# A four-pass exponential on VectorE, with a scaled copy of V made on GpSimd, in an attention kernel

## The chip, the cores and the metric

The kernel runs on one core of one Trainium2 chip. The metric is the device time of one execution in microseconds (us). The core has five engines that run their own instruction streams and meet at semaphores: TensorE (PE; its weight loads are shown as PEld), VectorE (DVE), ScalarE (ACT), GpSimd (POOL) and SyncE (SP, which only issues DMAs here).

## The reference

A residual layer: softmax attention with 16 heads of 28 columns, gated by a feed-forward branch. Both branches read the same normalised input.

```python
xn = _layernorm(x, axis=-1)                       # x: 1 x 2048 x 448
# attention
qkv = (xn @ wqkv).reshape(B, S, 3, 16, 28).transpose(2, 0, 3, 1, 4)
q, k, v = qkv[0], qkv[1], qkv[2]
p = softmax(einsum("bhqd,bhkd->bhqk", q, k) * 28 ** -0.5, axis=-1)
s = einsum("bhqk,bhkd->bhqd", p, v).transpose(0, 2, 1, 3).reshape(B, S, 448) @ wo
# feed-forward branch, 448 -> 1792 -> 448
h = gelu(xn @ w1 + b1)
g = silu(h @ w2 + b2)
out = x + s * g
```

## The kernel before

**Tiles.** Heads are handled in four head groups of four heads; a head takes 32 rows (28 and 4 of padding), so a head group fills 128 rows. Queries are handled in four chunks of 512, keys in 16 tiles of 128. A *block* is one head group with one chunk of queries; there are 16 blocks. Within a block a *tile* is the scores of one key tile (128 rows) against 512 queries of one head: 64 tiles in a block, 1024 in all, numbered by `m`. Four consecutive tiles (one key tile, four heads) are a *group*, numbered 0 to 255; block b has the groups 16b to 16b+15. In the last block the queries are cut: first half of the chunk, then a quarter and a quarter, so a tile there holds two or four key tiles side by side; `pieces` (line 1210) lists them.

**The main stream.** `p_scores` makes the scores of two or three tiles at a time (a unit) in PSUM banks of `ring`: three banks for one unit, two for the next, by turns. `p_exps` takes a unit's exponential on ScalarE (line 1293) into a slot of `P`, or, when they are free, of `h` and `xnT`. The scores of unit u wait until the exponential of unit u-2 is done. `p_pv` and `pv_task` multiply each exponential tile by the values (`vaug`, 28 columns and a column that yields the softmax's sum) and add the results of a block up in the PSUM bank `acc` (line 1508); four heads run beside each other in column strips of 32. At a block's end `p_epi` copies `acc` out (line 1566), and normalises by way of a reciprocal (line 1576), two small GpSimd instructions (lines 1578 and 1579), a product on PE (line 1588) and one on VectorE (line 1595). The next block's sums start in `acc` after the copy.

**The late groups.** `QUADS` (line 31) lists 35 groups whose exponential is not taken on ScalarE. Their scores go one tile at a time to whatever bank is free, alone or joined with a unit of the main stream (`p_late`), and VectorE writes from each tile a bfloat16 number whose bits are a scaled score (`p_apass`, line 1396): its exponent is the integer part of the score in base 2 and its mantissa the fraction, so that the tile T holds (1 + f) 2^e. `p_expq` corrects the fraction over all four tiles (128 x 2048) in five passes on VectorE:

- W keeps the mantissa under a fixed exponent (line 1447), so W = 2(1 + f);
- D1 = a W + b (line 1449);
- W = W D1 (line 1451);
- D1 keeps the exponent of T, 2^e (line 1452);
- W = W T (line 1454).

T, D1 and W are three of up to twelve *units* of memory that are free at the time (`x_sb`, `plx`, `w2`, `wq`, `wk`, `kT`). Their sum is the exponential; it isn't formed: `pv_task` multiplies all three by V, and PE adds them. So a late group costs three products with V where another costs one. One `p_expq` runs at a time (`K.ln2e`).

**Order.** The program is written by a planner: each process yields tasks with an engine, what they read and write, an estimated duration and a priority; `run` takes the task that can start first by the estimates and appends it to its engine's list, with the semaphore waits that `deps` derives. On the chip each engine runs its list strictly in order. `p_busy` adds products with a tile of zeros to `acc` (line 909) wherever the planner finds PE under 85% busy over 3.4 us.

**Other work.** Before and beside the main stream run the normalisation, the projections to q, k and v (lines 748 and 1039; v is written at line 1049), the first feed-forward product (line 1101), from block 8 the GELU (line 1150), then the second product (line 1171), the addition of `b2` on VectorE (line 1177), the gate (lines 1187 and 1191) and the output projection (lines 1605 and 1614). GpSimd issues the accumulating output DMAs (line 1622). All loads are issued by SP in the order of `loads`; `b2b`, a copy of `b2` for each partition, has a tile of its own.

Of the kernel before, what the change touches and what calls it, by code (L numbers as in the profile page):

```python
# [8 lines left out]
ALU = mybir.AluOpType  # L9
# [5 lines left out]
D = 448  # L15
# [4 lines left out]
C = 4  # L20
KT = 4
T = 16
# [5 lines left out]
MTOT = NBLK * T * 4  # L28

GM = 64 * 9 + 6  # L30
QUADS = (17, 18, 25, 37, 41, 58, 68, 70, 81, 90, 97, 98, 117, 124, 131, 135, 140, 142, 146, 154, 157, 159, 161, 162, 165, 183, 185, 197, 200, 210, 211, 225, 229, 234, 242)
SM_SCALE = DH ** -0.5
LOG2E = 1.4426950408889634
EXP_A3, EXP_A2, EXP_LC = 0.16391228, 0.00783292, 1.1187538523466403
EXP_OFF = 64.0 / (LOG2E * SM_SCALE)
LN_EPS = 1e-5
KNORM = 2.5
# [39 lines left out]
class _Kernel:  # L77
# [186 lines left out]
    def alloc(self):  # L264
        nc = self.nc
        f32, bf = dt.float32, dt.bfloat16
        sb = self.sb
# [27 lines left out]
        self.colK = sb("colK", [128, G], f32)  # L295
        self.plx = sb("plx", [128, 2048], bf)
        self.coff = sb("coff", [128, 1], f32)
        self.b2b = sb("b2b", [128, D], bf)
        self.st6 = sb("st6", [128, T, 6], f32)
        self.mv = sb("mv", [128, T, 2], f32)  # L300
        self.lnv = sb("lnv", [128, T], f32)
# [49 lines left out]
        self.b_qT = [[B() for _ in range(C)] for _ in range(G)]  # L351
        self.b_onT = self.b_qT
        self.q_ready = [[False] * C for _ in range(G)]
        self.b_v = [[B() for _ in range(T)] for _ in range(2)]
        self.b_h = [B() for _ in range(C)]
        self.b_g = [B() for _ in range(C)]
# [33 lines left out]
    def schedule(self):  # L390
        K = self
        K.n_f1 = 0
        K.exp_u = -1
        K.exp_m = -1
        K.late_ready = []
        K.sc_u = -1
        K.pv_m = -1
        K.E_done = -1
        K.norms_done = False
        K.stg_done = 0  # L400
        K.pe_wait = 0
# [12 lines left out]
        K.next_m = 0  # L414
        K.n_late = 0
        K.gu = None
        K.pend = None
        K.units = []
        K.pv_done = [False] * MTOT
        K.late = {4 * q + k for q in QUADS for k in range(4)}  # L420
        K.late_left = [sum(1 for q in QUADS if K.sub_of(4 * q) == b) for b in range(NBLK + 3)]
        K.late_on = False
        K.PB, K.PPREV, K.plast = {}, {}, {}
        K.free_u = []
        K.a_left = {}
        K.ln2e = 0
        K.late_blk = 0
        K.banks += [(K.ring[:, b, :], K.b_ring[b]) for b in (3, 2)]
        K.outs = []
        K.gelu_done = False  # L430
        K.dir_n = 0
        K.dir_read = 0
        self.constants()
        self.loads()
        for c in range(C):
            K.spawn(K.p_ln(c), c)
        K.spawn(K.p_first(), 0)
# [24 lines left out]
        for c in range(C):  # L462
            K.spawn(K.p_k(1, c), nxt())
        K.spawn(K.p_q(1, 0), nxt())
        for t in range(T):
            K.spawn(K.p_v1(t), nxt())
        for c in (1, 2, 3):
            K.spawn(K.p_q(1, c), nxt())
        K.spawn(K.p_qn(1), nxt())
        f1 = deque(SBT)  # L470
        for c in range(C):
            for _ in range(4):
                K.spawn(K.p_f1(*f1.popleft()), nxt())
            K.spawn(K.p_k(2, c), nxt())
            K.spawn(K.p_q(2, c), nxt())
        K.spawn(K.p_qn(2), nxt())
        while f1:
            K.spawn(K.p_f1(*f1.popleft()), nxt())
        for c in range(C):
            K.spawn(K.p_k(3, c), nxt())  # L480
            K.spawn(K.p_q(3, c), nxt())
        K.spawn(K.p_qn(3), nxt())
        K.spawn(K.p_gelu(), 0)
        K.spawn(K.p_direct(), 0)
        for c in range(C):
            for t in range(4):
                K.spawn(K.p_f2(c, t), nxt())
            K.spawn(K.p_silu(c), nxt())
        K.o_epi = 0.5
        for c in range(C - 1):  # L490
            for t in range(4):
                K.spawn(K.p_out(c, t), nxt())
        for t in range(4):
            K.spawn(K.p_last(t), nxt())
        K.run()
        for h in K.outs:
            K.wait(SP, h)
# [92 lines left out]
    def loads(self):  # L590
# [20 lines left out]
            ld(K.x_sb[:, c, :, :], xr[c], K.s_x[c], [K.b_x[c]], 8.0 + 1.8 * c)  # L611
        lw(4 * DH, D, K.s_wqk1, K.b_stg1, 16.5)

        ld(K.b2b[:, :], K.B_b2.partition_broadcast(128), K.s_w["b"], [K.b_b2], 20)
        ld(K.w1[:, 0:3, :], K.B_w1[0:384, :].rearrange("(kt p) f -> p kt f", p=128), K.s_w["w1"], [], 0)
        ld(K.w1[0:64, 3, :], K.B_w1[384:448, :], K.s_w["w1"], [K.b_w1], 30)

# [7 lines left out]
        def late_w2():  # L625
# [4 lines left out]
                    K.b_w2.r += b.r + [b.w]  # L630
            ld(K.w2[:, :, :], K.B_w2.rearrange("(ft p) d -> p ft d", p=128), K.s_w["w2"], [K.b_w2], K.now + 14)
        K.spawn(late_w2(), 50)

        def pool_pads():
            yield ("until", lambda: K.stg_done == 2)
# [525 lines left out]
    def p_f2(self, c, t):  # L1161
# [5 lines left out]
        for q in range(7):  # L1167
            def f(eng, q=q):
                ins = None
                for ft in (2 * q, 2 * q + 1):  # L1170
# [3 lines left out]
            yield _Task(PE, f, [K.b_w2, K.b_h[c]], [tok], 0.378, 0.17)  # L1174
        K.pe_wait -= 1
        fb = K.fsb[:, c % 2, t, :]
        yield _Task(DVE, lambda eng: eng.tensor_tensor(fb, ps, K.b2b[:, :], ALU.add), [tok, K.b_b2], [K.b_fsb[c % 2]],
                    0.63, 0.0, 2)
        K.banks.append((bank, tok))
        K.f2n[c] += 1  # L1180
# [251 lines left out]
    def p_expq(self, m0, u):  # L1432
        K = self
        b = K.sub_of(m0)
        uv = []
        yield ("until", lambda: K.ln2e == 0 and K.a_left[m0] == 0 and K.unit_of(b) is not None)
        K.ln2e = 1
        for _ in range(2):
            yield ("until", lambda: K.unit_of(b) is not None)
            v = K.unit_of(b)  # L1440
            K.free_u.remove(v)
            uv.append(v)
        K.late_blk = b
        u16, f16 = dt.uint16, dt.float16
        T, D1, W = K.unit[u], K.unit[uv[0]], K.unit[uv[1]]
        bT, bD, bW = K.b_U[u], K.b_U[uv[0]], K.b_U[uv[1]]
        yield _Task(DVE, lambda eng: eng.tensor_scalar(W.bitcast(u16), T.bitcast(u16), 0x407F, None, op0=ALU.bitwise_and),
                    bT, bW, 0.69, 0.0, 4)
        yield _Task(DVE, lambda eng: eng.tensor_scalar(D1.bitcast(f16), W, EXP_A3 / 4.0, EXP_A2 / 2.0, op0=ALU.mult, op1=ALU.add),
                    bW, bD, 0.69, 0.0, 4)  # L1450
        yield _Task(DVE, lambda eng: eng.tensor_tensor(W.bitcast(f16), W, D1.bitcast(f16), ALU.mult), bW + bD, bW, 1.22, 0.0, 4)
        yield _Task(DVE, lambda eng: eng.tensor_scalar(D1.bitcast(u16), T.bitcast(u16), 0x7F80, None, op0=ALU.bitwise_and),
                    bT + bW, bD, 0.69, 0.0, 4)
        yield _Task(DVE, lambda eng: eng.tensor_tensor(W, W.bitcast(f16), T, ALU.mult), bT + bW, bW, 1.22, 0.0, 4)
        K.ln2e = 0
        K.late_ready.append((m0, (u, uv[0], uv[1])))

    def p_pv(self):
        K = self
# [27 lines left out]
    def pv_task(self, q, late, ms):  # L1487
# [2 lines left out]
        for x in late:  # L1490
            K.late_ready.remove(x)
        K.late_left[b] -= len(late)
        src = [(m,) + K.p_slot(m) for m in ms if m not in K.late]
        for m0, us in late:
            for u in us:
                src += [(m0 + k, K.unit[u][:, 512 * k:512 * k + 512], K.b_U[u][k]) for k in range(4)]
        n = len(src) / 4
        fl, rd = [], []
        for kk in range(4):
            for m, ap, tok in src:  # L1500
                _, j, pc, _, s = K.pieces(m)
                g = q // 16 // C
                if kk >= len(pc):
                    continue
                t, q0, nq, col = pc[kk]

                def f(eng, t=t, j=j, g=g, q0=q0, nq=nq, col=col, ap=ap):
                    return eng.matmul(K.acc[32 * j:32 * j + 32, q0:q0 + nq], K.vaug[:, t, 4 * g + j, :],  # L1508
                                      ap[:, col:col + nq], tile_position=(0, 32 * j), start=(t == 0),
                                      stop=(t == T - 1), skip_group_check=True)  # L1510
                fl.append(f)
                rd += [tok, K.b_v[0 if g == 0 else 1][t]]

        if not src:
            return
# [1 line left out]
        def fall(eng, fl=fl):  # L1517
            ins = None
            for f in fl:
# [1 line left out]
            return ins  # L1521
        yield _Task(PE, fall, rd, [K.b_acc], 0.223 * n + 0.001 * len(fl), 0.17,
                    lambda: 1.2 if K.exp_m - K.pv_m > 20 or K.exp_m > MTOT - 12 or (K.gu is not None and K.gu - 1 <= K.exp_u <= K.gu) else 6, mode="col")
        for _, us in late:
            K.free_u += us

    def p_slot(self, m):
        i = self.PB[m]
# [170 lines left out]
```

## Time and profile before

| what | value |
|---|---|
| median of 4 runs | 459.8 us (459.69 to 460.25) |
| the profiled execution's own time | 460.08 us |
| its span, first to last instruction | 458.3 us |
| granted TensorE clock, mean | 0.998 of full speed |
| first exponential of the main stream starts | 12.99 us |
| end of block 0, 3, 7, 8, 11, 14 (copy of `acc`, line 1566) | 46.6, 128.3, 234.2, 274.8, 356.2, 432.6 us |

The page of the profile gives each engine's busy time, its share of the span and its number of instructions, then the busy share in 40 equal slices of the span as digits (9 is 90% or more). A group of instructions is named by the line of the kernel that issues it, the engine, the operation, what is written and read, the shape and the count; behind the first bar stand its busy time in us and the mean duration of one in ns, behind the second the idle time of its engine just before it and what ended most of that. A table of waits has who waited, for whom, the sum in us, the times and the longest. A window has its length and then busy time and count of PE, PEld, DVE, ACT and POOL, the clock, the DMA share and GB/s. Durations of neighbours on one engine can overlap by some 0.1 us.

### The profile page before, as it was taken

The page shows a single profiled execution, that of the slowest core. Times are in us where ns is not written, and L with a number is a line of the kernel's source. Part 1 is how long each engine was busy: PE and PEld are TensorE (multiplying, and loading weights), DVE is VectorE, ACT ScalarE, POOL GpSimd, SP SyncE. Part 2 cuts the span into 40 slices and gives each one's busy share as a digit, 9 for nine tenths or more (in the row PEclk, how much of TensorE's full clock was granted, in tenths as well). Part 3 has the DMA queues.
Part 4 walks back from the last instruction along what each step waited for, and adds up shares of the span by engine and source line. Part 5 has one row for each costly group of instructions (what it writes and reads, how often), then busy time and mean ns, then how long its engine had stood idle before and what let it go on. Part 6 is the DMA issues. An engine that isn't in the chain of part 4 may idle for free.

```text
span 458.3 us, 10703 instructions
## 1 busy us (share of the span) xinstructions
PE 437.6 (95%) x4475; PEld 164.5 (36%) x4475; DVE 381.6 (83%) x593; ACT 445.3 (97%) x406; POOL 44.9 (10%) x85
## 2 busy tenths in 40 slices
PE   6999999999999999999999999999999999999995
PEld 5543334332233233223234333333233333343562
DVE  8956988885878888968899899889878798889865
ACT  5999999999999999999999999999999999999994
POOL 7471000000000100100000001010000100111012
PEclk9999999999999999999999999999999999999999
DMA  8701000000000000000040000000000000402012
GB/s 270 268 2 37 2 0 1 1 1 4 1 0 1 1 2 2 3 1 1 0 139 5 2 0 1 2 1 1 0 1 2 1 1 1 82 1 33 11 23 62
DMA packets 8050, 11.16 MB, mean 24 GB/s; under 512 B 1698, under 2 KB 6994, under 8 KB 7955
## 3 DMA queue, kind: packets, MB, share of 16 engines
q1 hardware_dynamic: 6850, 8.43, 5.9%
q0 software_dynamic: 864, 1.38, 2.3%
q8 instruction: 35, 0.57, 0.5%
q10 hardware_dynamic: 288, 0.69, 0.4%
q14 instruction: 13, 0.10, 0.1%
HBM read 8.61 MB, written 3.21 MB: 26 GB/s over the span
## 4 chain that ended last, share of the span: by engine, by line
PE 55%; ACT 31%; issue 11%; DVE 2%; POOL 1%; ACTq 0%; DVEq 0%; POOLq 0%
PE ring L1237 16%; ACT P L1293 14%; PE acc L1508 9%; ACT xnT L1293 7%; ACT h L1293 7%; PE ring L1101 6%; PE ring L1171 4%; PE acc L909 4%; PE ring L748 3%; PE misc L1101 2%; PE misc L748 2%; PE misc L1039 1%; ACT h L1150 1%; PE misc L1171 1%; PE acc L891 1%
## 5 line engine op out<-in xcount | busy, mean ns | idle before, releaser
L1293 ACT ACTIVATE P<-ring 128x1024 bf16<-128x1024 f32 (+1 forms) x186 | 214.9, 1270 | 1.4 <-PE ring L1237 1.3
L1237 PE MATMUL ring<-qT,kT 32*128 32x512 bf16 (+2 forms) x1075 | 145.4, 358 | 10.9 <-ACT P L1293 3.9
L1293 ACT ACTIVATE h<-ring 128x1024 bf16<-128x1024 f32 (+1 forms) x103 | 118.5, 1244 | 0.4 <-PE ring L1237 0.2
L1237 PEld LDWEIGHTS ring<-qT,kT 32*128 32x128 bf16 x1075 | 37.5, 91 | 133.0 <-ACT P L1293 52.7
L1293 ACT ACTIVATE xnT<-ring 128x1536 bf16<-128x1536 f32 (+1 forms) x71 | 82.4, 1285 | 0.1
L1508 PE MATMUL acc<-P,vaug 128*32 128x512 bf16 (+2 forms) x526 | 48.4, 356 | 0.0
L1101 PE MATMUL ring<-xnT,w 128*128 128x512 bf16 x164 | 43.1, 382 | 0.2 <-ACT h L1150 0.2
L1578 POOL CAST rhi<-rc 128x16 bf16<-128x16 f32 x15 | 5.9, 393 | 357.6 <-DVE rc L1576 333.7
L1171 PE MATMUL ring<-w,h 128*128 128x448 bf16 x154 | 37.4, 355 | 0.0
L909 PE MATMUL acc<-ident,zero 128*128 128x128 bf16 x429 | 35.0, 220 | 0.0
L909 PEld LDWEIGHTS acc<-ident,zero 128*128 128x128 bf16 x429 | 24.3, 98 | 15.4 <-issue 14.6
L1237 PE MATMUL misc<-qT,kT 32*128 32x512 bf16 (+1 forms) x77 | 28.7, 377 | 0.0
L1508 PE MATMUL acc<-h,vaug 128*32 128x512 bf16 x250 | 28.0, 384 | 0.0
L1396 DVE TENSOR_SCALAR x_sb<-ring 128x512 uint16<-128x512 f32 x26 | 17.9, 687 | 2.8 <-PE ring L1237 2.6
L1101 PEld LDWEIGHTS ring<-xnT,w 128*128 128x128 bf16 x164 | 12.3, 97 | 20.1 <-issue 7.7
L1508 PE MATMUL acc<-xnT,vaug 128*32 128x512 bf16 (+2 forms) x232 | 18.1, 333 | 0.0
L1508 PEld LDWEIGHTS acc<-P,vaug 128*32 128x32 bf16 x526 | 12.0, 94 | 16.0 <-issue 13.4
L1171 PEld LDWEIGHTS ring<-w,h 128*128 128x128 bf16 x154 | 11.2, 97 | 17.1 <-issue 10.3
L1566 DVE CAST E_sb<-acc 128x512 bf16<-128x512 f32 x15 | 10.4, 691 | 8.3 <-PE acc L1508 8.3
L1101 PE MATMUL misc<-xnT,w 128*128 128x512 bf16 x60 | 17.2, 383 | 0.0
L1396 DVE TENSOR_SCALAR kT<-misc 128x512 uint16<-128x512 f32 x20 | 13.8, 688 | 4.1 <-PE misc L1237 4.1
L1396 DVE TENSOR_SCALAR x_sb<-misc 128x512 uint16<-128x512 f32 x22 | 15.1, 686 | 2.4 <-PE misc L1237 2.1
(281 smaller groups left out, 686.1 us busy)
## 6 DMA issues: line engine op xcount, KB each, us to landing
w<-in_B_w_dram SPq DMA_DIRECT2D x1, 1568.0 KB, 7.3
w<-in_B_w_dram SPq DMA_DIRECT2D x1, 1344.0 KB, 8.6
out_dram<-in_A_x_dram SPq DMA_DIRECT2D x3, 448.0 KB, 10.4
out_dram<-h POOLq DMA_DIRECT2D x6, 224.0 KB, 3.8
x_sb<-in_A_x_dram SPq DMA_DIRECT2D x2, 448.0 KB, 4.5
h<-in_A_wqkv_dram SPq DMA_DIRECT2D x3, 168.0 KB, 4.8
x_sb<-in_A_x_dram ACTq DMA_DIRECT2D x1, 448.0 KB, 4.1
h<-in_A_x_dram SPq DMA_DIRECT2D x1, 448.0 KB, 3.4
```

What stands on the lines that cost most here:

```text
L748: ins = eng.matmul(bank, w[:, kt, g * 128:(g + 1) * 128], K.xnT[:, kt, c * 512:(c + 1) * 512], start=(kt == 0), stop=(kt == KT - 1))
L891: yield _Task(PE, lambda eng: eng.matmul(bank[:, 0:256], K.ident[:, :], K.E_sb[:, 0, 0:256], start=True, stop=True), [K.b_id, K.b_pads], [ ...
L909: ins = eng.matmul(K.acc[:, 0:128], K.zero[:, :], K.ident[:, :], start=False, stop=True, skip_group_check=True)
L1039: ins = eng.matmul(bank[:, off:off + nh * 32], K.xnT[:, kt, t * 128:(t + 1) * 128], ap, start=(kt == 0), stop=(kt == KT - 1), skip_group_c ...
L1101: ins = eng.matmul(bank, K.w1[:, kt, ft * 128:(ft + 1) * 128], K.xnT[:, kt, c * 512:(c + 1) * 512], start=(kt == 0), stop=(kt == KT - 1))
L1171: ins = eng.matmul(ps, hv[:, ft, t * 128:(t + 1) * 128], K.w2[:, ft, :], start=(ft == 0), stop=(ft == FT - 1))
L1237: return eng.matmul(dst, K.kT[32 * j:32 * j + 32, g, t * 128:(t + 1) * 128], K.qT[32 * j:32 * j + 32, g, c * 512 + q0:c * 512 + q0 + nq], ...
L1293: return eng.activation(reg[:, i0:i0 + n, :], K.ring[:, b0:b0 + n, :], ACTF.Exp, scale=SM_SCALE)
L1396: yield _Task(DVE, lambda eng: eng.tensor_scalar(K.unit[u][:, 512 * k:512 * k + 512].bitcast(dt.uint16), bank, SM_SCALE * LOG2E * 128.0, ( ...
L1508: return eng.matmul(K.acc[32 * j:32 * j + 32, q0:q0 + nq], K.vaug[:, t, 4 * g + j, :], ap[:, col:col + nq], tile_position=(0, 32 * j), sta ...
L1566: yield _Task(DVE, lambda eng: eng.tensor_copy(E, K.acc[:, :]), [K.b_acc], [tE], 0.7, 0.0, 0)
L1578: yield _Task(POOL, lambda eng: eng.tensor_copy(K.rhi[:, :], K.rc[:, :]), [K.b_rc], [K.b_rhl], 1.1, 0.0, 1)
```

## The change

The exponential of the late groups becomes 2^e (1 + (1 + f) + C (1 + f)^3), with a cube in place of the quadratic and cubic terms, in four passes: W keeps the mantissa as before; D1 = W W; W = D1 T; D1 keeps the exponent of T. The factor C/4 isn't applied to the tiles: for each piece of a late group, GpSimd makes a copy of the four heads' values times C/4 (`p_cv`), 128 x 128, and the product of W with V takes the copy in place of `vaug`. There are four such copies (`cv`); a group's chain starts only when one is free and the values it copies are written. The list has 38 groups in place of 35, at other places for the most part: blocks 3, 11 and 12 have one more each, the other blocks as many as before.

To make room for `cv`, `b2b` is put into the memory of `wv` (the weights of v), and its load is issued by SP once all of v is written.

```diff
-QUADS = (17, 18, 25, 37, 41, 58, 68, 70, 81, 90, 97, 98, 117, 124, 131, 135, 140, 142, 146, 154, 157, 159, 161, 162, 165, 183, 185, 197, 200, 210, 211, 225, 229, 234, 242)
+QUADS = (17, 19, 21, 34, 41, 49, 53, 70, 74, 87, 88, 99, 108, 113, 114, 131, 135, 138, 141, 146, 149, 152, 157, 161, 162, 169, 177, 178, 184, 194, 195, 201, 212, 219, 226, 227, 236, 242)
...
-EXP_A3, EXP_A2, EXP_LC = 0.16391228, 0.00783292, 1.1187538523466403
+EXP_C, EXP_LC = 0.1669921875, 1.1155446
+NCV = 4
...
-        self.b2b = sb("b2b", [128, D], bf)
+        self.b2b = self.wv[:, 0, 0:D]
+        self.cv = sb("cv", [128, NCV, 128], bf)
...
-        ld(K.b2b[:, :], K.B_b2.partition_broadcast(128), K.s_w["b"], [K.b_b2], 20)
...
+        def late_b2():
+            yield ("until", lambda: all(x.tw is not None for x in K.b_v[1]))
+            K.b_b2.r += K.b_wv.r + K.b_wvpad.r + [K.b_wv.w, K.b_wvpad.w]
+            ld(K.b2b, K.B_b2.partition_broadcast(128), K.s_w["b"], [K.b_b2], K.now + 6)
+        K.spawn(late_b2(), 50)
...
-        yield ("until", lambda: K.ln2e == 0 and K.a_left[m0] == 0 and K.unit_of(b) is not None)
+        _, _, pc, _, _ = K.pieces(m0)
+        bv = K.b_v[0 if m0 // 64 < C else 1]
+        room = lambda: [i for i in range(0, NCV, len(pc)) if all(k in K.free_cv for k in range(i, i + len(pc)))]
+        yield ("until", lambda: K.ln2e == 0 and K.a_left[m0] == 0 and K.unit_of(b) is not None and room()
+               and all(bv[p[0]].tw is not None for p in pc))
         K.ln2e = 1
+        cs = list(range(room()[0], room()[0] + len(pc)))
+        for i in cs:
+            K.free_cv.remove(i)
+        g = m0 // 64 // C
+        K.spawn(K.p_cv(cs, [p[0] for p in pc], g, bv), m0)
...
-        yield _Task(DVE, lambda eng: eng.tensor_scalar(D1.bitcast(f16), W, EXP_A3 / 4.0, EXP_A2 / 2.0, op0=ALU.mult, op1=ALU.add),
-                    bW, bD, 0.69, 0.0, 4)
-        yield _Task(DVE, lambda eng: eng.tensor_tensor(W.bitcast(f16), W, D1.bitcast(f16), ALU.mult), bW + bD, bW, 1.22, 0.0, 4)
+        yield _Task(DVE, lambda eng: eng.tensor_tensor(D1.bitcast(f16), W, W, ALU.mult), bW, bD, 1.22, 0.0, 4)
+        yield _Task(DVE, lambda eng: eng.tensor_tensor(W, D1.bitcast(f16), T, ALU.mult), bT + bD, bW, 1.22, 0.0, 4)
         yield _Task(DVE, lambda eng: eng.tensor_scalar(D1.bitcast(u16), T.bitcast(u16), 0x7F80, None, op0=ALU.bitwise_and),
                     bT + bW, bD, 0.69, 0.0, 4)
-        yield _Task(DVE, lambda eng: eng.tensor_tensor(W, W.bitcast(f16), T, ALU.mult), bT + bW, bW, 1.22, 0.0, 4)
...
+    def p_cv(self, cs, ts, g, bv):
+        K = self
+        for i, t in zip(cs, ts):
+            yield _Task(POOL, lambda eng, i=i, t=t: eng.tensor_scalar(
+                K.cv[:, i, :], K.vaug[:, t, 4 * g:4 * g + 4, :].rearrange("p h e -> p (h e)"), EXP_C / 4.0, None, op0=ALU.mult),
+                [bv[t]], [K.b_cv[i]], 0.35)
...
+                w = K.vaug[:, t, 4 * g + j, :] if cs is None else K.cv[:, cs[kk], 32 * j:32 * j + 32]
...
-                rd += [tok, K.b_v[0 if g == 0 else 1][t]]
+                rd += [tok, K.b_v[0 if g == 0 else 1][t] if cs is None else K.b_cv[cs[kk]]]
```

More of the change, by code (lines that the diff above doesn't have):

```diff
@@ L353, in alloc @@
         self.q_ready = [[False] * C for _ in range(G)]
+        self.b_cv = [B() for _ in range(NCV)]
         self.b_v = [[B() for _ in range(T)] for _ in range(2)]
@@ L424, in schedule @@
         K.free_u = []
+        K.free_cv = list(range(NCV))
         K.a_left = {}
@@ L1176, in p_f2 @@
         fb = K.fsb[:, c % 2, t, :]
-        yield _Task(DVE, lambda eng: eng.tensor_tensor(fb, ps, K.b2b[:, :], ALU.add), [tok, K.b_b2], [K.b_fsb[c % 2]],
+        yield _Task(DVE, lambda eng: eng.tensor_tensor(fb, ps, K.b2b, ALU.add), [tok, K.b_b2], [K.b_fsb[c % 2]],
                     0.63, 0.0, 2)
@@ L1448, in p_expq @@
                     bT, bW, 0.69, 0.0, 4)
-        yield _Task(DVE, lambda eng: eng.tensor_scalar(D1.bitcast(f16), W, EXP_A3 / 4.0, EXP_A2 / 2.0, op0=ALU.mult, op1=ALU.add),
-                    bW, bD, 0.69, 0.0, 4)
-        yield _Task(DVE, lambda eng: eng.tensor_tensor(W.bitcast(f16), W, D1.bitcast(f16), ALU.mult), bW + bD, bW, 1.22, 0.0, 4)
+        yield _Task(DVE, lambda eng: eng.tensor_tensor(D1.bitcast(f16), W, W, ALU.mult), bW, bD, 1.22, 0.0, 4)
+        yield _Task(DVE, lambda eng: eng.tensor_tensor(W, D1.bitcast(f16), T, ALU.mult), bT + bD, bW, 1.22, 0.0, 4)
         yield _Task(DVE, lambda eng: eng.tensor_scalar(D1.bitcast(u16), T.bitcast(u16), 0x7F80, None, op0=ALU.bitwise_and),
                     bT + bW, bD, 0.69, 0.0, 4)
-        yield _Task(DVE, lambda eng: eng.tensor_tensor(W, W.bitcast(f16), T, ALU.mult), bT + bW, bW, 1.22, 0.0, 4)
         K.ln2e = 0
-        K.late_ready.append((m0, (u, uv[0], uv[1])))
+        K.late_ready.append((m0, (u, uv[0], uv[1]), cs))
+    def p_cv(self, cs, ts, g, bv):
[4 more added lines that the diff above has]
+                [bv[t]], [K.b_cv[i]], 0.35)
     def p_pv(self):
@@ L1492, in pv_task @@
         K.late_left[b] -= len(late)
-        src = [(m,) + K.p_slot(m) for m in ms if m not in K.late]
-        for m0, us in late:
+        src = [(m,) + K.p_slot(m) + (None,) for m in ms if m not in K.late]
+        for m0, us, cs in late:
             for u in us:
-                src += [(m0 + k, K.unit[u][:, 512 * k:512 * k + 512], K.b_U[u][k]) for k in range(4)]
+                src += [(m0 + k, K.unit[u][:, 512 * k:512 * k + 512], K.b_U[u][k], cs if u == us[2] else None) for k in range(4)]
         n = len(src) / 4
@@ L1499, in pv_task @@
         for kk in range(4):
-            for m, ap, tok in src:
+            for m, ap, tok, cs in src:
                 _, j, pc, _, s = K.pieces(m)
@@ L1505, in pv_task, with f @@
                 t, q0, nq, col = pc[kk]
-                def f(eng, t=t, j=j, g=g, q0=q0, nq=nq, col=col, ap=ap):
-                    return eng.matmul(K.acc[32 * j:32 * j + 32, q0:q0 + nq], K.vaug[:, t, 4 * g + j, :],
+                w = K.vaug[:, t, 4 * g + j, :] if cs is None else K.cv[:, cs[kk], 32 * j:32 * j + 32]
+                def f(eng, t=t, j=j, w=w, q0=q0, nq=nq, col=col, ap=ap):
+                    return eng.matmul(K.acc[32 * j:32 * j + 32, q0:q0 + nq], w,
                                       ap[:, col:col + nq], tile_position=(0, 32 * j), start=(t == 0),
@@ L1523, in pv_task @@
                     lambda: 1.2 if K.exp_m - K.pv_m > 20 or K.exp_m > MTOT - 12 or (K.gu is not None and K.gu - 1 <= K.exp_u <= K.gu) else 6, mode="col")
-        for _, us in late:
+        for _, us, cs in late:
             K.free_u += us
+            K.free_cv += cs
     def p_slot(self, m):
```

## The prediction

> **What bounds the kernel now.** I read the page's busy shares and slices first, to see which engine is full and where.
>
> ```profile
> span 458.3 us, 10703 instructions
> ...
> PE 437.6 (95%) x4475; PEld 164.5 (36%) x4475; DVE 381.6 (83%) x593; ACT 445.3 (97%) x406; POOL 44.9 (10%) x85
> ...
> DVE  8956988885878888968899899889878798889865
> ACT  5999999999999999999999999999999999999994
> ```
>
> ACT (ScalarE) is full in all slices but the first and the last. DVE (VectorE) stands at eight or nine tenths. The busy PE (TensorE) is not proof of a bound: 35.0 us of it are the products with `zero` of line 909, filler that the planner sets where it finds PE idle. So I asked for the busy time of the stretch between start-up and tail:
>
> ```profile
> 20.00:450.00 430.00, 419.04 (x4307) 152.87 (x4304) 359.83 (x528) 428.49 (x375) 30.49 (x50) 1.00 0.05 11
> ```
>
> After the length stand PE, weight load, DVE, ACT, POOL (GpSimd). ACT rests 1.5 us of 430; DVE rests 70.2. The chain of waits must agree, and at first sight it does not:
>
> ```profile
> PE 55%; ACT 31%; issue 11%; DVE 2%; POOL 1%; ACTq 0%; DVEq 0%; POOLq 0%
> ...
> PEld ring L1237 <- ACT P L1293: 52.7, 131, 0.7
> ```
>
> More than half of the chain is PE, but the second line, from the table of waits, says what PE waits for before scores: 131 times for an exponential to release the ring. With the same rows of tiles `h` (30.8) and `xnT` (21.3) that is 104.8 us. Scores and exponentials hand the same banks to and fro; the one that never rests, ACT, sets the pace. What a score tile costs ACT I read from its instructions in order of time:
>
> ```profile
> 98.89 1.46 ACT L1293 ACTIVATE P<-ring 128x1536 bf16<-128x1536 f32 x1
> 100.22 1.04 ACT L1293 ACTIVATE h<-ring 128x1024 bf16<-128x1024 f32 x1
> 101.13 6.01 ACT L1293 ACTIVATE P<-ring 128x1536 bf16<-128x1536 f32 x5
> ```
>
> Starts lie 1.33 us apart for three tiles and 0.91 for two, less than the durations, as neighbours overlap. Five tiles take 2.24 us: 0.448 per tile.
>
> **ScalarE's share.** There are 1024 tiles; 35 groups of four are VectorE's, so ScalarE has 884; with 38 groups it has 872. Twelve tiles by 0.448 are **5.4 us** off the full engine. A check from the whole: the stream from the first exponential (12.99) to its last (451.54) is 438.5; less 27.3 of GELU, 2.6 of table loads behind the first and 6.4 of tanh it leaves 402 us for 884 tiles, 0.455 each, or 5.5. I take 5.4.
>
> **VectorE's passes.** The rows of one group:
>
> ```profile
> L1396 DVE TENSOR_SCALAR kT<-misc 128x512 uint16<-128x512 f32 x20 | 13.8, 688 | 4.1 <-PE misc L1237 4.1
> L1451 DVE TENSOR_TENSOR kT<-kT,x_sb 128x2048 f16<-128x2048 bf16 x6 | 7.3, 1217 | 0.0
> L1454 DVE TENSOR_TENSOR kT<-kT,x_sb 128x2048 bf16<-128x2048 f16 x5 | 6.1, 1217 | 0.0
> L1452 DVE TENSOR_SCALAR x_sb<-w 128x2048 uint16<-128x2048 uint16 x7 | 4.8, 685 | 0.0
> L996 DVE TENSOR_TENSOR qsq<-qT 128x512 bf16<-128x512 bf16 x15 | 6.3, 419 | 0.4
> ```
>
> Before: four L1396 (2.75), three one-input passes L1447, L1449, L1452 at 0.69 (2.07), two products at 1.22 (2.44): 7.26 us. The new chain drops the pass of L1449 and keeps two products: 6.57. The new square of W has one tensor as both inputs; L996 is such a product, and (1217 - 419)/1536 = 0.52 ns per element joins the two sizes on one line, so I cost it at 1.22. In all 38 x 6.57 = 249.7 against 35 x 7.26 = 254.1: **4.4 us less work on VectorE**, though three groups more. It buys nothing by itself, as DVE rests; it is the room for the groups.
>
> **GpSimd's scaled copy.** 37 groups have one piece and group 242 two: 39 instructions of 128x128. No such row exists. From below, the copy of 128x128 (line 575) took 0.29; from above, the two-scalar form on f32 (line 567) 0.83. Between 128x4 (0.24, line 704) and 128x448 (0.76, line 714) a line gives 0.39, which I take as nearest in kind. That is 15.2 us on an engine that is busy 10%. The chain of a group now also waits for one of four free copies; as a group holds three of at most twelve units until it is added, four in flight are the most there were, and I cost this at nothing (a missing copy would cost a wait until an older group is added, on VectorE, which rests). The copy starts with the chain of passes, which needs 0.69 + 1.22 + 1.22 + 0.69 = 3.8 us before PE may use it. But GpSimd and VectorE do not run beside each other freely:
>
> ```profile
> L710 DVE TENSOR_SCALAR h<-x_sb,mv,rstd x10: 364/396/789, 6.0 to 27.2; 128x448 bf16<-128x448 bf16 x10
> ...
> L1578 POOL CAST rhi<-rc x15: 196/529/652, 49.8 to 434.7; 128x16 bf16<-128x16 f32 x15
> L1579 POOL TENSOR_TENSOR rlo<-rc,rhi x15: 217/543/1209, 50.1 to 435.3; 128x16 bf16<-128x16 f32 x15
> ```
>
> The numbers are shortest, median and longest. The 1.21 of L1579 at 183.82 began 0.09 after a VectorE product of 1.22 and ended with it; the 0.79 of L710 lay beside a GpSimd product of 0.93 and is twice its median. So a copy may wait 1.2 us and then hold a VectorE pass. Late: 1.2 + 0.39, with both lines 1578 and 1579 ahead of it in GpSimd's queue at their longest (1.86), 3.45 us, still under 3.8. From block 13 on an output DMA issue (line 1622, up to 1.18) can be ahead too; then PE waits 0.8 us at its products with the exponentials, and the next scores are queued behind them. Held: from 0, since around 183 the next VectorE pass began as usual, to 39 x 0.39 = 15.2 us of VectorE time, 3.4 points of its share.
>
> The Trainium skill, "SBUF — State Buffer", section "SBUF: two separate sides", says that the pair of ports which VectorE shares with GpSimd goes to one of them for a whole instruction, and that the other is blocked until it ends. It speaks against moving anything beside VectorE's passes. The rows agree in kind (0.79 against 0.40); by the rule taken to its end the upper bound of 15.2 us is the price on VectorE, by the rows around 183 nearly nothing.
>
> **TensorE.** A late group has three products with V for one: 24 more, at 0.76 us for 12 (the chain's pieces at line 1508) 1.5 us. Twelve scores leave the units for single ones: at most 12 x 0.22 = 2.6 (line 1508's sets of four start at 318.35, 318.56 and 318.78, and a score is as wide), less 12/2.5 = 4.8 units of 0.22: 1.1. Sum 3.0 us, half hidden under filler or more. Where filler lacks, ScalarE pays: bounds 0 to 3.0.
>
> **b2.** Its load leaves SP's queue at 8.22 (0.59 us of issue) and returns once the last v is written (line 1049, about 97 us), before the `qT<-qst` of 109. It took 6.2 us; its first reader, line 1177, comes at 281. Cost nothing; were that cover gone, 6.2 us.
>
> **Sum.** Profiled execution 460.08, span 458.3, median of the runs 459.8. The span becomes 458.3 - 5.4 = 452.9. For held passes and fuller PE I add 0.4, an estimate: ScalarE lost 1.5 us in 430 with VectorE at 83%, and I let that grow by a quarter. 453.3 of span, 455.1 for its own execution, and against the median **454.8 us**.
>
> **Rivals.** The three extra groups fall into blocks 3, 11 and 12 (the other changes shift groups within a block). The ends of the blocks are line 1566's copies; their windows:
>
> ```profile
> 102.10:128.30 26.20, 25.85 (x226) 7.39 (x224) 19.11 (x29) 26.18 (x24) 0.41 (x2) 1.00 0.01 3
> 331.30:356.20 24.90, 24.88 (x239) 8.24 (x235) 20.15 (x28) 24.90 (x22) 0.41 (x2) 1.00 0.01 2
> 356.20:380.80 24.60, 24.45 (x237) 8.21 (x234) 21.06 (x30) 24.55 (x22) 1.20 (x2) 1.00 0.01 1
> ```
>
> *TensorE takes over there.* For: filler in these blocks is 0.00, 0.68 and 1.19 us. Against: filler of 9.9 us in 402 to 433, to which the second feed-forward product (last at 386) can drift. All 3.0 us lost: 457.4.
>
> *VectorE becomes the bound in those blocks* and the sign turns. A block cannot end before its last group is added into `acc`, and PE stands in order there with the next scores behind it. Blocks 11 and 12 hold 41.2 us of VectorE; less 4 x 0.69, plus 2 x 6.57, that is 51.6 in 49.5 - 3.6 = 45.9 us: 5.7 too much. Block 3: 19.1 - 1.4 + 6.6 = 24.3 in 24.4, just full. Held passes of eight groups add 3.1. Price 8.8: **463.2 us**. It decides once more than 5.4 of this reaches ScalarE. Against: of blocks 11 and 12 some 10 us are other work (seven L1177 of 0.62, four L1191 of 1.09, two L1595 of 0.69), bound to no block's end; from 381 to 450 VectorE rests 11 us and is relieved of 4.
>
> *No change*: the passes become fewer but the plan leaves ScalarE 5.4 us of gaps through all blocks, 0.14 us per group: 459.8. Against: single waits of PE for VectorE before its products are at most 0.4 us.
>
> **How the numbers follow.** Forecast 0.60, TensorE 0.12, no change 0.06, VectorE bound 0.22. A measurement tells 0.2% (0.9 us) from no change: faster 0.72, within 0.05 (a near miss of either sign can pass it), slower 0.23. The low end: 454.4 less the 1.5 us ScalarE now rests is 452.9, so 453.0. Up to 457.4 the range covers the forecast and TensorE, and to 461.5 no change and a third of the last rival's cases: about 0.16 left out. The forecast's own range is 453.0 to 456.5.
>
> **What would show it.** ScalarE's exponentials must sum to 872 tiles and its rest between 20 and 445 stay under 2.5 us; a rest of 7 or more means that I am wrong, and its releaser says by whom: scores behind PE's line 1508 waiting for VectorE, or for GpSimd's copy. VectorE's busy time should fall to about 377 us; the square should take 1.22 us, the copy 0.39 alone and up to 1.6 when it waits. Passes of 0.69 that last 1.0 or more in the copies' shadow would prove the upper bound of the hold. Line 1177 should shift later than 386 by some us.

## The result, and the profile after

The kernel after takes **460.89 us** (median of 30 runs, 460.30 to 461.42) against 459.81 before (48 runs): a ratio of 1.0022, 95% interval [1.0017, 1.0027]. The forecast was 454.8, faster; it is 1.1 us slower. The profiled execution took 460.89.

First the page after, its busy shares and the slices of the two engines that were read before; then the stretch of 430 us:

```profile
span 459.4 us, 10832 instructions
PE 437.2 (95%) x4505; PEld 166.0 (36%) x4505; DVE 374.5 (82%) x582; ACT 440.9 (96%) x401; POOL 76.6 (17%) x124
...
DVE  8956898979678698789788988388988988798955
ACT  5999999999999999999999999999999999999992
```

```profile
20.00:450.00 430.00, 418.73 (x4339) 154.54 (x4337) 352.37 (x516) 425.13 (x371) 61.65 (x88) 1.00 0.05 11
```

VectorE has less to do (352.4 of 430 us, before 359.8), ScalarE too, but the last exponential ends only 0.9 us sooner (450.73, before 451.65): ScalarE's rest in this stretch grew from 1.5 to 4.9 us, between the two marks of the prediction (under 2.5 if right, 7 or more if wrong). The page says who ended it. Busy time and mean stand behind the first bar, the rest just before behind the second; first the kernel before, then after:

```profile
L1293 ACT ACTIVATE P<-ring 128x1024 bf16<-128x1024 f32 (+1 forms) x186 | 214.9, 1270 | 1.4 <-PE ring L1237 1.3
L1293 ACT ACTIVATE h<-ring 128x1024 bf16<-128x1024 f32 (+1 forms) x103 | 118.5, 1244 | 0.4 <-PE ring L1237 0.2
L1293 ACT ACTIVATE xnT<-ring 128x1536 bf16<-128x1536 f32 (+1 forms) x71 | 82.4, 1285 | 0.1
```

```profile
L1302 ACT ACTIVATE P<-ring 128x1024 bf16<-128x1024 f32 (+1 forms) x186 | 214.3, 1261 | 2.2 <-PE ring L1246 1.0
L1302 ACT ACTIVATE h<-ring 128x1024 bf16<-128x1024 f32 (+1 forms) x101 | 116.5, 1233 | 1.8 <-PE ring L1246 1.0
L1302 ACT ACTIVATE xnT<-ring 128x1536 bf16<-128x1536 f32 (+1 forms) x68 | 79.6, 1286 | 0.6 <-PE ring L1246 0.2
```

The exponentials (line 1293 before, 1302 now) waited 4.6 us, before 1.9, and where the page names what ended a wait it is scores (line 1237 before, 1246 now). The chain of waits, with more of TensorE in it (67%, before 55%), and the table of waits show the other side:

```profile
PE 67%; ACT 22%; issue 7%; DVE 3%; POOL 1%; ACTq 0%; DVEq 0%; POOLq 0%
```

```profile
PEld ring L1246 <- ACT P L1302: 50.4, 127, 0.8
PEld ring L1246 <- ACT h L1302: 30.8, 74, 0.7
...
PEld ring L1246 <- ACT xnT L1302: 15.9, 40, 1.3
```

TensorE waited for an exponential 241 times (97.1 us); before 256 times (104.8). Five of the 15 fewer go with the five units fewer; in the rest TensorE is no longer the one that waits.

**Where the time went.** I cut each profiled execution in three: up to the first exponential, from there to the end of the last (the stream), and the rest up to the execution's own time. In the stream I sum the spacing of two starts on ScalarE less 1.333 us behind an exponential of three tiles and less 0.906 behind one of two ("late starts"; shorter spacings count as negative), and take GELU's 17 instructions from the first start to the start of what follows them.

| kernel | start | stream | end | late starts | GELU |
|---|---|---|---|---|---|
| before | 13.0 | 438.7 | 8.4 | 8.1 | 25.3 |
| after | 13.1 | 437.7 | 10.2 | 11.5 | 26.1 |

The start is not a difference of the kernels: over all profiles here it lies between 12.5 and 13.2 us.

Five units are gone, two of three tiles and three of two: 2 x 1.333 + 3 x 0.906 = 5.4 us, just as forecast. Late starts gave back 3.4, and GELU 0.8, where its last instruction waits for a first feed-forward product (0.68 us); so the stream is only 1.0 shorter. Behind the last exponential 1.7 us were added. Put down to the blocks by the copies of `acc` that end them in each kernel, 3.0 of these 4.2 us came in blocks 5, 6 and 7 and about 1 in block 9 (most of it GELU's), which have as many late groups as before; blocks 3, 11 and 12, which have one more each, lost 0.7 (1.2, if each exponential is counted to the block of its tiles). The other blocks together were 0.5 us shorter. The largest late starts follow exponentials that start at 180, 203.8, 222.5 and 228 (0.6 to 0.7 us each) and, within GELU, 273 (0.8). The first of them, first ScalarE, then TensorE (start, duration, instructions):

```profile
180.17 1.12 ACT L1302 ACTIVATE h<-ring 128x1024 bf16<-128x1024 f32 x1
181.70 1.45 ACT L1302 ACTIVATE h<-ring 128x1536 bf16<-128x1536 f32 x1 [0.41 <-PE misc L1246]
```

```profile
179.52 0.61 PE L1110 MATMUL ring<-xnT,w 128*128 128x512 bf16 x2
180.06 0.62 PE L1533 MATMUL acc<-h,vaug 128*32 128x512 bf16 x8
180.50 0.39 PE L1533 MATMUL acc<-x_sb,vaug 128*32 128x512 bf16 x4
180.72 0.39 PE L1533 MATMUL acc<-w,vaug 128*32 128x512 bf16 x4
180.93 0.39 PE L1533 MATMUL acc<-w,cv 128*32 128x512 bf16 x4
181.25 0.39 PE L1246 MATMUL ring<-qT,kT 32*128 32x512 bf16 x3
```

TensorE doesn't wait here. Two products of the feed-forward branch, eight with exponentials and the late group's twelve stand in its list ahead of the next scores, and ScalarE rests 0.41 us until these are there. The products with the scaled copy (`cv`) are the last of this row, but they wait for nobody. At the other three places of the stream a late group's products stand just ahead of the scores as well, and at none of the four does a product with zeros.

### The profile page after: what moved, and what is told of

Same layout as the page of the kernel before. It is cut to its first block, busy times and chain, and to the rows that moved or that the text cites. A ratio compares the mean times of both kernels' runs of the same rounds, so it can differ in the third digit from the quotient of the medians.

```text
span 459.4 us, 10832 instructions
## 1 busy us (share of the span) xinstructions
PE 437.2 (95%) x4505; PEld 166.0 (36%) x4505; DVE 374.5 (82%) x582; ACT 440.9 (96%) x401; POOL 76.6 (17%) x124
## 4 chain that ended last, share of the span: by engine, by line
PE 67%; ACT 22%; issue 7%; DVE 3%; POOL 1%; ACTq 0%; DVEq 0%; POOLq 0%
PE ring L1246 18%; ACT P L1302 15%; PE acc L1533 13%; PE ring L1110 7%; PE ring L1180 5%; ACT xnT L1302 4%; PE misc L1110 4%; PE ring L757 3%; ACT h L1302 3%; PE misc L1180 3%; PE acc L918 3%; PE misc L757 2%; PE misc L1048 1%; PE ring L1048 1%; PE ring L1631 1%
## 5 line engine op out<-in xcount | busy, mean ns | idle before, releaser
L1246 PE MATMUL ring<-qT,kT 32*128 32x512 bf16 (+2 forms) x1074 | 143.0, 358 | 10.2 <-ACT P L1302 4.6
L1302 ACT ACTIVATE h<-ring 128x1024 bf16<-128x1024 f32 (+1 forms) x101 | 116.5, 1233 | 1.8 <-PE ring L1246 1.0
L1302 ACT ACTIVATE xnT<-ring 128x1536 bf16<-128x1536 f32 (+1 forms) x68 | 79.6, 1286 | 0.6 <-PE ring L1246 0.2
L1477 POOL TENSOR_SCALAR cv<-vaug 128x128 bf16<-128x128 bf16 x39 | 30.6, 785 | 158.5 <-PE acc L1533 156.6
L1110 PE MATMUL ring<-xnT,w 128*128 128x512 bf16 x152 | 39.3, 381 | 0.0
L1180 PE MATMUL ring<-w,h 128*128 128x448 bf16 x126 | 29.9, 355 | 0.2 <-DVE rc L1602 0.2
L1533 PE MATMUL acc<-h,vaug 128*32 128x512 bf16 x245 | 28.1, 385 | 0.0
L1405 DVE TENSOR_SCALAR x_sb<-ring 128x512 uint16<-128x512 f32 x31 | 21.2, 685 | 4.9 <-PE ring L1246 4.8
L1180 PE MATMUL misc<-w,h 128*128 128x448 bf16 x98 | 23.9, 355 | 0.0
L1110 PE MATMUL misc<-xnT,w 128*128 128x512 bf16 x72 | 20.0, 382 | 0.0
L1405 DVE TENSOR_SCALAR x_sb<-misc 128x512 uint16<-128x512 f32 x25 | 17.1, 684 | 2.6 <-PE misc L1246 2.5
```

Source lines behind the costliest of these rows:

```text
L1110: ins = eng.matmul(bank, K.w1[:, kt, ft * 128:(ft + 1) * 128], K.xnT[:, kt, c * 512:(c + 1) * 512], start=(kt == 0), stop=(kt == KT - 1))
L1180: ins = eng.matmul(ps, hv[:, ft, t * 128:(t + 1) * 128], K.w2[:, ft, :], start=(ft == 0), stop=(ft == FT - 1))
L1246: return eng.matmul(dst, K.kT[32 * j:32 * j + 32, g, t * 128:(t + 1) * 128], K.qT[32 * j:32 * j + 32, g, c * 512 + q0:c * 512 + q0 + nq], ...
L1302: return eng.activation(reg[:, i0:i0 + n, :], K.ring[:, b0:b0 + n, :], ACTF.Exp, scale=SM_SCALE)
L1405: yield _Task(DVE, lambda eng: eng.tensor_scalar(K.unit[u][:, 512 * k:512 * k + 512].bitcast(dt.uint16), bank, SM_SCALE * LOG2E * 128.0, ( ...
L1477: yield _Task(POOL, lambda eng, i=i, t=t: eng.tensor_scalar(K.cv[:, i, :], K.vaug[:, t, 4 * g:4 * g + 4, :].rearrange("p h e -> p (h e)"), ...
```

## The experiments

Theory: TensorE is late with scores since its one list of instructions, which it runs in order, puts too much between them at places that the new list of groups made. Rivals: GpSimd's copies beside VectorE's passes; VectorE's passes; the three extra groups in blocks 3, 11 and 12; the end alone. Unless it says otherwise, a kernel starts from the one after and keeps its planned order. Each stood beside runs of the kernel before on the same chip (459.84 to 459.87).

**The copies left out** (W is multiplied by V without its factor):

```diff
-        K.spawn(K.p_cv(cs, [p[0] for p in pc], g, bv), m0)
...
-                src += [(m0 + k, K.unit[u][:, 512 * k:512 * k + 512], K.b_U[u][k], cs if u == us[2] else None) for k in range(4)]
+                src += [(m0 + k, K.unit[u][:, 512 * k:512 * k + 512], K.b_U[u][k], cs if False else None) for k in range(4)]
```

> The changed kernel without GpSimd's 39 scaled copies: the product of W takes the plain values, so the factor C/4 on the cube is left out; every other instruction stands in the same order on its engine. Theory 'TensorE is full, its order makes the scores late': same time as the changed kernel, 460.9 within 0.6 us, and ScalarE's gaps between 13 and 450 us stay near 4.8 us. Rival 'the copies hold VectorE's passes and PE waits for them': at least 2 us faster, under 459, and the gaps fall to about 2 us.

Measured: 460.74, ratio 1.0018 [1.0009, 1.0028]; the stream is 437.7 and the late starts 11.5, as after. All 39 copies together are worth 0.15 us by the medians, which is within the noise.

**One pass cut to 128 of 2048 columns** (2^e of the other columns is left out), 18 us less VectorE work:

```diff
-        yield _Task(DVE, lambda eng: eng.tensor_scalar(D1.bitcast(u16), T.bitcast(u16), 0x7F80,
+        yield _Task(DVE, lambda eng: eng.tensor_scalar(D1.bitcast(u16)[:, 0:128], T.bitcast(u16)[:, 0:128], 0x7F80,
```

> The changed kernel with the pass that keeps the exponent done on 128 of 2048 columns, so the rest of D1 is left as it was; every instruction in the same place and with the same waits. VectorE has 38 x 0.55 = 21 us less to do. Theory 'TensorE is full': 460.9 within 0.6 us. Rival 'VectorE is the bound in the blocks with an extra group': at least 2 us faster, under 459.

Measured: 461.02, 1.0025 [1.0016, 1.0035]. Its stretch of 430 us shows VectorE at 334.3 in place of 352.4 and ScalarE as it was:

```profile
20.00:450.00 430.00, 418.71 (x4339) 154.70 (x4340) 334.28 (x516) 425.12 (x372) 60.96 (x88) 1.00 0.05 11
```

ScalarE's stream is 437.7 as after. VectorE is not the bound.

**Two of a late group's three products with V left out** (those of T and D1), the order and the planned durations kept:

```diff
-                fl.append(f)
+                if m in K.late and cs is None:
+                    skipped += 1
+                else:
+                    fl.append(f)
```

> The changed kernel with two of a late group's three sets of products (those of T and D1 with V) left out of PE's program, so the sums lack them; every other instruction stands in the same order with the same waits. PE has some 300 products fewer, 19 us of its stream. Theory 'TensorE is full, runs of 20 products hold the scores': ScalarE's gaps fall from 4.8 to under 2.5 us and the time by 2 to 4 us, to 457-459. Rival 'VectorE is the bound': gaps and time as in the changed kernel, 460.9 within 0.6.

Measured: **457.74**, 0.9953 [0.9938, 0.9968]; stream 434.8, late starts 9.0, ScalarE's rest after the start 2.85 us (4.82 after; the bound I had set was a little too low). The same place as above, now without the late group's eight products for T and D1:

```profile
179.09 2.55 ACT L1302 ACTIVATE h<-ring 128x1024 bf16<-128x1024 f32 x2
181.53 1.02 ACT L1302 ACTIVATE P<-ring 128x1024 bf16<-128x1024 f32 x1
```

ScalarE goes through. So the lost time lies on TensorE's path. But 312 products went, in sets of four at 0.22 us some 17 us of TensorE's work, to win 3.1: most of this work stood where it cost nothing.

**The last output projection of chunk 2 put ahead** (its priority in the plan, 2 in place of 5):

```diff
-        yield K.t_wo(ps, tok, c, t, (0, 1))
+        yield K.t_wo(ps, tok, c, t, (0, 1), 2 if c == C - 2 else 5)
```

> The changed kernel with a higher priority for the output projection of chunk 2 (its products before those of chunk 3 in PE's order). Theory 'the end comes 1.6 us later because the last accumulating output DMA, which GpSimd issues, waits for the last piece of chunk 2': the DMA is issued before 450 and the time falls by 1.3 to 1.8 us to about 459.3; the exponentials end within 0.5 us of before. Rival 'the end is set by chunk 3 anyway': 460.9 within 0.4.

Measured: 459.92, 1.0001 [0.9992, 1.0011], 1.0 us less than after (I had expected 1.3 to 1.8); the stream is the same (437.8). GpSimd's last instructions, first of the kernel after, then of this one:

```profile
451.27 1.07 POOL L1214 TENSOR_TENSOR h<-w 128x448 bf16<-128x448 bf16 x1 [6.54 <-ACT w L1212]
452.42 1.03 POOL L1216 TENSOR_TENSOR h<-h,w 128x448 bf16<-128x448 bf16 x1
454.64 0.88 POOL L1648 DMA_DIRECT2D out_dram<-h  x1 [1.19 <-DVE h L1644]
```

```profile
447.88 0.86 POOL L1648 DMA_DIRECT2D out_dram<-h  x1 [3.69 <-DVE h L1640]
450.91 1.03 POOL L1214 TENSOR_TENSOR h<-w 128x448 bf16<-128x448 bf16 x1 [2.17 <-ACT w L1212]
452.02 1.06 POOL L1216 TENSOR_TENSOR h<-h,w 128x448 bf16<-128x448 bf16 x1
```

After the change GpSimd's last accumulating output DMA is issued behind the last gate, at 454.64 (before: 449.34). It lands at 458.33, and SyncE's last output DMA, issued beside it at 455.63, lands at 458.65, 3.02 us after its issue; before the change, and here with GpSimd's out of the way, that one takes 1.65 us. These late landings account for most of the 1.7 us that the end lost. Not all comes back here, as the last work ahead of SyncE's DMA stretches (5.35 us from the last exponential to its issue, 4.90 after, 4.51 before). That end was a second loss, which no step of the prediction had.

**The same two products left out for some groups only**: those added to blocks 3, 11 and 12 (49, 178, 195), or six of blocks 5 to 7 (87, 88, 99, 108, 113, 114).

```diff
-                if m in K.late and cs is None:
+                if m // 4 in (49, 178, 195) and cs is None:
```

> The changed kernel with the products of T and D1 left out for three groups alone, 49, 178 and 195, one each in blocks 3, 11 and 12, so the sums lack those terms; order and waits as in the changed kernel; PE has 24 products fewer, the 1.5 us that the three extra groups were priced at. If the loss is the extra groups' own load on TensorE, the time falls by 1 to 1.5 us to 459.4-459.9. If it comes from where the order stands tight elsewhere, 460.9 within 0.4.

> The same leaving-out for the six groups of blocks 5 to 7 (87, 88, 99, 108, 113, 114), where the largest late starts of ScalarE stand (0.4 to 0.7 us at 181, 205, 224 and 229); 48 products fewer. If TensorE has no time left just there, these late starts shrink and the time falls by 1.5 to 2.5 us to 458.4-459.4. If the late starts come from waits that stand in the order (a bank, a pass), less than 0.5 us.

Measured: 460.80, 1.0021 [1.0012, 1.0030] for the three; 459.47, 0.9994 [0.9985, 1.0002] for the six, late starts 10.4. The 24 products left out of the three added groups, as many as the change added, cost nothing that can be told from noise; the 48 of six groups that were only shifted cost 1.4 us (a little less than I had expected), nearly half of what the whole set brought.

**The same two products left out of the kernel before** (there the condition asks for T and D1 by their units):

> The kernel before with the products of T and D1 left out for all 35 late groups; order and waits as before; 280 products fewer. Its ScalarE rests 1.4 us between 13 and 450 us against 4.8 in the changed kernel. If the order before had fitted TensorE's load to ScalarE's pace, there is little to gain: 458.3 to 459.3, against the 3.1 us that the same leaving-out gave in the changed kernel. If TensorE's load bounds both alike, about 456.7.

Measured: 458.72, 0.9975 [0.9965, 0.9985]; late starts 6.8. Before the change the same relief (288 products) is worth 1.1 us, after it (312) 3.1. As the 24 products of the three added groups are worth nearly nothing, I put the difference of 2.0 us down to the new order, not to the load as such.

**Four passes on before's list of 35 groups**:

> The changed kernel with the list of 35 groups of the kernel before: four passes, GpSimd's copies, b2 moved, but ScalarE has its 884 tiles. If time saved on VectorE were worth anything by itself, or cost nothing, the time is that of before, 459.8 within 0.5, or less. If what matters is an order on TensorE fitted to the passes, a list fitted to five passes is late with four: 461.5 to 463.5, and ScalarE's gaps are over 4 us though it has no tile less.

Measured: 464.21, 1.0092 [1.0079, 1.0106], beyond the range that I gave. Less VectorE work (334.9 of 430 us), the same 360 units, and 4.4 us slower: late starts 9.7 (8.1 before), and GELU 28.1 us (25.3), where ScalarE waits for single products of TensorE, once for 1.23 us. On this list the shorter chain alone is a loss: units and products are as many as before, and the copies cost nothing on the other list; what differs is the order.

**Five passes on the new list of 38 groups**:

> Before's five passes with the change's list of 38 groups: the fourth corner beside before (459.8), the change (460.9) and four passes on before's list (464.2). Theory (a list is fitted to one chain's order, and VectorE's five passes at 7.26 us a group leave no room for three more): 465 us or more, ScalarE's gaps over 8 us. Rival (the list alone makes the time, the chain nothing): 460 to 462 us.

Measured: 483.71, 1.0518 [1.0502, 1.0535]. The groups of exponentials with their rests:

```profile
L1293 ACT ACTIVATE P<-ring 128x1024 bf16<-128x1024 f32 (+1 forms) x186 | 215.3, 1261 | 15.8 <-PE acc L1508 13.1
L1293 ACT ACTIVATE h<-ring 128x1024 bf16<-128x1024 f32 (+1 forms) x101 | 116.5, 1264 | 2.9 <-PE acc L1508 2.1
L1293 ACT ACTIVATE xnT<-ring 128x1536 bf16<-128x1536 f32 (+1 forms) x68 | 79.6, 1274 | 7.8 <-PE acc L1508 7.3
```

ScalarE rests 26.5 us, mostly behind products with V. Its longest rest, with the VectorE pass ahead of them:

```profile
314.81 1.22 DVE L1454 TENSOR_TENSOR wq<-wq,wk 128x2048 bf16<-128x2048 f16 x1
```

```profile
314.07 1.17 PE L909 MATMUL acc<-ident,zero 128*128 128x128 bf16 x18
315.07 1.30 PE L1171 MATMUL ring<-w,h 128*128 128x448 bf16 x6
316.30 0.39 PE L1508 MATMUL acc<-P,vaug 128*32 128x512 bf16 x2
```

```profile
317.67 1.02 ACT L1293 ACTIVATE P<-ring 128x1024 bf16<-128x1024 f32 x1 [5.46 <-PE acc L1508]
```

VectorE ends a group at 316.03, the block's last products with V follow at 316.30 with the next scores behind them, and the list has TensorE busy with zeros and other work until then. This is the rival of a VectorE bound, as the prediction drew it, but with five passes. On the same list four passes take 460.9: they do make the room for 38 groups.

**Four passes, 38 groups, another list**, with the projection put ahead as above. Groups were moved about until the planner's own estimates left ScalarE fewer late starts; each block has as many groups as after the change.

```diff
-QUADS = (17, 19, 21, 34, 41, 49, 53, 70, 74, 87, 88, 99, 108, 113, 114, 131, 135, 138, 141, 146, 149, 152, 157, 161, 162, 169, 177, 178, 184, 194, 195, 201, 212, 219, 226, 227, 236, 242)
+QUADS = (16, 20, 25, 35, 37, 54, 56, 68, 78, 86, 91, 96, 105, 113, 123, 132, 135, 137, 142, 151, 155, 156, 157, 160, 162, 171, 176, 179, 186, 193, 197, 206, 211, 215, 224, 225, 233, 242)
```

> Four passes, 38 groups, with the last rows' projection of chunk 2 ahead in the order as in the tail run, and another list of 38 groups: groups were moved about until the order left ScalarE fewer late starts. Only which groups are VectorE's is changed by that, not how many. Theory (five units fewer are worth their 5.4 us, and the changed order of TensorE gives them back as late starts, so another list with the same load keeps most of them): 454.5 to 457.5 us, ScalarE's gaps under 3.5 us, last exponential before 448.5. Rival (TensorE is full whatever the list, the 38 groups can't be had): 459 to 461, gaps 4.5 or more as after the change.

Measured: **456.21**, 0.9920 [0.9907, 0.9934]: faster than both kernels. Its exponentials on the page:

```profile
L1302 ACT ACTIVATE P<-ring 128x1024 bf16<-128x1024 f32 (+1 forms) x186 | 214.5, 1269 | 1.1 <-PE ring L1246 0.8
L1302 ACT ACTIVATE h<-ring 128x1024 bf16<-128x1024 f32 (+1 forms) x101 | 116.1, 1247 | 1.0 <-PE ring L1246 0.5
L1302 ACT ACTIVATE xnT<-ring 128x1536 bf16<-128x1536 f32 (+1 forms) x68 | 79.5, 1300 | 0.0
```

The rest before them is 2.1 us (after: 4.6), with the same units and as many scores and products with V; only products with zeros are fewer (375, after: 435). Start 12.6, stream 434.9, end 8.7; late starts 8.0, the figure of before. GELU takes 27.0 (before: 25.3), so of the 5.4 us of exponentials 3.7 are kept. The run that differs by the list alone is the one above with the projection ahead, 459.92: the list is worth 3.7 us, most of it in the stream (434.9 against 437.8).

**Controls for it**: before's five passes and 35 groups with a list searched in the same way and for as long; and the four passes with a rule of order besides: no TensorE task of over 0.7 us is begun when scores could start within 0.3 us (again with a list of its own).

```diff
+            if E == PE and p[3].dur > 0.7 and p[3].prio > 1:
+                hot = [c for c in cand if c[1][3].E == PE and c[1][3].prio <= 1 and c[0] <= s + 0.3]
```

> Control for the run with four passes and a list of its own: before's five passes and 35 groups, with a list that was moved about in the same way and for as long. Theory (the four passes are what allows the saving; before's list stands near its best): 457.8 to 459.5 us. Rival (a better list alone brings it, the four passes nothing): within 1 us of the run with four passes.

> As the run with four passes and a list of its own, and with the order written so that a run of TensorE work of over 0.7 us isn't begun when a tile of scores could start within 0.3 us (an own list of 38 groups found under that rule). Theory: the late starts behind runs of products with V shrink, 454 to 457.5 us, late starts above 0.4 us fewer than after the change. Rival (the late starts are the load's, not the order's): no faster than 459.

Measured: 460.22, 1.0009 [1.0000, 1.0017] for five passes, above the range that I gave: the search found nothing there, and 4.0 us lie between the two. (This control hasn't the projection ahead, but with an end of 8.5 us in its profile it has nothing to win by it.) With the rule 457.37, 0.9944 [0.9931, 0.9956]: inside its range at the upper end, one late start above 0.4 us beyond the start-up (1.32 at 271, within GELU), but no better than the other list alone. The rule isn't needed, or not in this form.

## Why the prediction was wrong

- **ScalarE's share** held: 5.4 us of exponentials are gone.
- **VectorE's passes** held: 374.5 us busy (about 377 forecast), the square 1.21 to 1.22 us. VectorE as the bound in blocks 11 and 12 did not come: 18 us less of its work change nothing. In that rival's sum block 3 was wrong, without consequence: its window holds one chain of passes, not two, so it comes to 25.0 in 24.4 us, not 24.3.
- **GpSimd's copy** was mis-sized without harm: 0.53 us alone (0.39 forecast), up to 1.55 when it waits (1.6 forecast). No one-input pass of 2048 columns took more than 0.78 us and no product more than 1.33, so the hold of up to 15.2 us is not there; neither is a wait of TensorE for a copy.
- **b2** costs nothing: its reader's instructions start between 279.5 and 383.2. That it would shift later than 386 was wrong.
- **TensorE is the step that failed**: "3.0 us, half hidden under filler or more". It counted the work that is added and laid it upon the old order. What came is 4.2 us (3.4 of late starts and 0.8 in GELU), above the upper bound, and not from the added products: 24 products of the three added groups are worth nothing, 48 of six shifted groups 1.4, and with another list the same work leaves 8.0 us of late starts in place of 11.5. Neither the sum nor a rival had the new order itself as a term; TensorE's rival placed the price in blocks 3, 11 and 12, where 0.7 (or 1.2) of it lies. The added 0.4 us "for held passes and fuller PE" let ScalarE's rest grow by a quarter; it went from 1.43 to 4.82 us after the start.
- **The end** was taken to move with the stream. It lengthened by 1.7 us, most of it through one late output projection, whose DMA, with the last one beside it, lands late; putting that ahead brings 1.0 back. The sum had nothing for it.

The reckoning: 5.4 saved, 4.2 given back in the stream, 1.7 at the end, 0.1 at the start make 0.6 us slower; the two profiled executions differ by 0.8, the medians by 1.1. *No change* came nearest, by its mechanism too (the plan leaves gaps), but through all blocks by 0.14 us a group it was not: the price sits at a few places.

What stays open: why just this list has those places. That it is the order is shown (same counts in each block, another list, 456.2 against 459.9, both with the projection ahead). Whether a still better list exists is open, and so is why GELU takes longer in all the four-pass kernels (25.7 to 28.1 us, before 25.3).

## What to carry over

Where a planner writes the whole program's order, a shorter chain doesn't remove its own time and leave the rest in place: every start moves, and an engine that is 95% busy in a fixed order is late wherever a long run lands ahead of what the full engine needs. Count then, beside the work, the late starts at the full engine and what ends last, and search the placement anew with the changed kernel before judging the change: here that was, with the projection put ahead, 3.7 us under the kernel before, in place of 1.1 over it.

## What the runs showed of the hardware

A one-input GpSimd instruction on 128x128 bfloat16 takes 0.53 us, more than the line through GpSimd's other shapes gave (0.39). A copy took up to 1.55 us when it met a pass; 13 of the 16 longer ones ended 0.38 or 0.39 us after the end of a VectorE instruction that was running. VectorE's passes beside copies lost about 0.1 us at most (one-input 0.78 in place of 0.69, a product 1.33 in place of 1.22). So between copies and passes it was GpSimd that paid; in the start-up, before any copy, a VectorE pass of the normalisation (line 719) still took up to 0.78 us against a median of 0.39.

```profile
L1477 POOL TENSOR_SCALAR cv<-vaug x39: 527/528/1552, 50.5 to 428.1; 128x128 bf16<-128x128 bf16 x39
L1469 DVE TENSOR_SCALAR plx<-kT x6: 678/684/695, 252.6 to 430.5; 128x2048 uint16<-128x2048 uint16 x6
```

SyncE's last output DMA took 2.9 to 3.4 us from issue to landing in the seven kernels that issue GpSimd's accumulating DMA about 1 us ahead of it, and 1.65 to 1.68 us in the seven others. Why isn't shown.
